# A new order of TensorE's work in the attention part and the first two experts of an xLSTM and mixture-of-experts kernel

## The chip, the cores and the metric

The kernel runs on one core of a Trainium2 chip. The metric is device time in microseconds of one execution; the time of the kernel before is the median of three runs.

## The reference

Three layers follow each other. The first is a gated linear attention (mLSTM) over 2 batches, 8 heads, 768 steps and a head size of 40. The second is a dense mixture of 4 experts over 1536 tokens, the third a top-1 mixture of 8 experts.

```python
# attention, per head and step t
C = f_stab * C + i_stab * outer(v_t, k_t)
n = f_stab * n + i_stab * k_t
y_t = sigmoid(o_t) * (C @ q_t) / max(abs(n @ q_t), 1.0)
# dense experts: x is (1536, 320), w1 (4, 320, 1024), w2 (4, 1024, 320)
p = domain_probs / (domain_probs.sum(-1, keepdims=True) + 1e-09)
out += p[:, e:e+1] * (np.maximum(x @ w1[e], 0.0) @ w2[e])     # for e in range(4)
# routed experts: one expert of 8 for each token, by the largest logit of x @ w_gate
out[i] = gate_w[i] * (np.maximum(disp @ w1[e], 0.0) @ w2[e])[pos[i]]
```

## The kernel before, in words

The sequence is cut into 12 chunks of 128 steps, 6 for each batch; chunk u gives token tile u of the experts. Chunks 0 to 3 run in float32. From chunk 4 on, operands are split into two float16 parts, high and low.

**Work items.** The attention and the first two experts (0 and 1) make up 48 + 24 items, and each has a place in one list, `SEQ`:

- `("S", u)`: the scores of chunk u (`scores32`, L1115, or `scores`, L1119). Ahead of it stand the broadcast of the chunk's maxima (L997) and the decay arguments (L1068 or L1075).
- `("B", u)`: the rest of chunk u: the product with the carried state (`inter`, L1205, L1215), with the values (`intra`, L1210, L1241), and the state's update (L1273, L1279).
- `("L", k, t)`: layer 1 of expert k on token tile t, in two halves of 32 matmuls (L644).
- `("M", k, t)`: layer 2 of the same, in two halves of 12 matmuls of 320 columns (L656).

**The planner.** `Sched` takes all operations of all engines with a guessed duration and their dependences. TensorE's operations have a due place, which for the items above is their index in `SEQ`. `urgency` turns these into latest starts, `starts` lays out a plan with all engines and the DMA queue, and `run` emits each engine's instructions in the plan's order. So the list sets not only TensorE's order: it moves the instructions of VectorE, ScalarE, GpSimd and the SP queue with it. On each engine the emitted order is kept.

**Fillers.** Where the plan has an idle stretch on TensorE in the first part (due place up to `FILLED = 45.0`), `gaps` puts matmuls on zeros there (`warm`, L416), 128x256 each; the plan's idle time after that place gets none.

**The way of one chunk from 4 on (`front`).** VectorE takes the maxima of q, k and v (L972), GpSimd reduces them over the partitions (L979), TensorE broadcasts the result into bank x3 (L997). VectorE reads that bank and makes power-of-two scales (`pow2_scale`, L442, L447, L452). ScalarE writes the high parts (L1027) and VectorE the low parts (L1033), q first, then k. SP issues a DMA transpose (L1039), and then the scores can run. After the scores VectorE multiplies by the decay (L1163), ScalarE rounds (L1176), GpSimd takes the rest (L1180), and `intra` can run.

**Other lines that the prediction names.** L665 is VectorE's low part of layer 1's output, L697 its sum into the output of a tile; L697 also sets free one of the two banks po0 and po1 that layer 2 writes. L589 and L594 split the weights of an expert into high and low float16 (`w_conv`), L551 broadcasts a weight maximum. L632 is the DMA transpose of a token tile, L422 any plain load.

Of the kernel before, what the change touches and what calls it, by code (L numbers as in the profile page):

```python
# [21 lines left out]
B, H, S, D = 2, 8, 768, 40  # L22
# [227 lines left out]
def xlstm_moe_kernel(ctx: ExitStack, tc: tile.TileContext, a, cap: int):  # L250
# [255 lines left out]
    wscale = lambda k, m: (wsm[:, k, m - 1, 8:9], wsm[:, k, m - 1, 9:10])  # L506

    SEQ = {x: i for i, x in enumerate((
 ("S", 0), ("B", 0), ("S", 1), ("B", 1), ("L", 0, 0), ("S", 2), ("L", 0, 1), ("M", 0, 1), ("B", 2), ("S", 3), ("L", 0, 2), ("B", 3), ("M", 0, 0), ("L", 1, 0), ("L", 1, 2), ("M", 1, 0), ("S", 4), ("M", 0, 2), ("L", 1, 1), ("B", 4), ("L", 0, 3), ("M", 1, 2), ("L", 1, 3), ("S", 5), ("L", 0, 4), ("S", 6), ("B", 5), ("M", 0, 4), ("L", 0, 5), ("S", 7), ("B", 6), ("M", 1, 1), ("L", 1, 5), ("B", 7), ("M", 0, 3), ("L", 1, 4), ("S", 8), ("B", 8), ("L", 0, 6), ("M", 0, 5), ("M", 1, 3), ("S", 9), ("B", 9), ("L", 0, 7), ("L", 0, 8), ("L", 1, 6), ("S", 10), ("M", 0, 7), ("L", 1, 9), ("M", 1, 6), ("M", 0, 8), ("M", 0, 6), ("L", 0, 10), ("B", 10), ("L", 0, 9), ("L", 1, 8), ("L", 1, 7), ("M", 0, 10), ("M", 1, 5), ("L", 1, 10), ("S", 11), ("M", 1, 8), ("M", 1, 4), ("B", 11), ("L", 0, 11), ("L", 1, 11), ("M", 1, 7), ("M", 0, 9), ("M", 1, 9), ("M", 1, 10), ("M", 1, 11), ("M", 0, 11),
    ))}  # L510
    at3 = NT * 10.0 + 50
    SPREAD_AT = {
# [1514 lines left out]
```

## Time and profile before

| | us |
|---|---|
| median of 3 runs (494.47 to 496.36) | 496.05 |
| the profiled execution, its own time | 495.52 |
| its span, first to last instruction | 493.8 |
| PE busy (96% of the span) | 475.5 |
| DVE busy (69%) | 340.6 |
| ACT busy (63%) | 311.9 |
| POOL busy (27%) | 131.7 |
| first matmul of expert 2, L644 with 512 columns | 196.07 |

The span has four parts: attention and experts 0 and 1 (to about 196 us), experts 2 and 3 with the routing, the routed experts, and a tail of scattered stores. The page sums engines over the whole span; the change acts on the first part, so its stretches have to be asked for apart.

### The profile page before, as it was taken

How to read it: one execution, taken by the hardware profiler on the slowest of the kernel's cores; microseconds unless marked ns; L12 is line 12 of the kernel's file. 1: busy time of each engine (PE TensorE's matmuls, PEld its weight loads, DVE VectorE, ACT ScalarE, POOL GpSimd, SP SyncE). 2: the span in 40 equal slices, each digit the busy share in tenths (PEclk: the TensorE clock that was granted, in tenths of full speed). 3: DMA queues.
4: the chain of work that ended last, by engine and by line, in shares of the span. 5: the costliest groups of instructions: out<-in, count | busy, mean ns of one | idle time of the engine just before them, and what ended most of it. 6: DMA issues, size and time to landing. Idle time of an engine off the chain costs nothing. (4 is left out here: it accounts for less than half of the span.)

```text
span 493.8 us, 13708 instructions
## 1 busy us (share of the span) xinstructions
PE 475.5 (96%) x5487; PEld 365.7 (74%) x5487; DVE 340.6 (69%) x972; ACT 311.9 (63%) x666; POOL 131.7 (27%) x243
## 2 busy tenths in 40 slices
PE   8999999999989899999999999999999999999994
PEld 6998978868868797886564746556564698888883
DVE  5898988799999834663968594879899982222120
ACT  1997979577687854856765568778879550322230
POOL 4751143665865410200010010000414111311111
PEclk9999999999999999999999999999999999999999
DMA  6996683354533796818686967628293545999200
GB/s 229 315 236 195 155 286 77 77 131 102 105 60 73 201 342 205 230 26 288 204 296 220 333 215 298 211 75 222 70 223 109 133 184 79 302 219 322 103 27 25
DMA packets 70772, 88.90 MB, mean 180 GB/s; under 512 B 48641, under 2 KB 56307, under 8 KB 70702
## 3 DMA queue, kind: packets, MB, share of 16 engines
q1 hardware_dynamic: 69502, 84.23, 59.4%
q0 software_dynamic: 1200, 3.73, 2.0%
q8 instruction: 45, 0.74, 0.6%
q14 instruction: 25, 0.20, 0.2%
HBM read 55.89 MB, written 21.70 MB: 157 GB/s over the span
## 5 line engine op out<-in xcount | busy, mean ns | idle before, releaser
L656 PEld LDWEIGHTS <-arena 128*128 128x128 f16 (+1 forms) x1416 | 136.4, 98 | 55.0 <-issue 3.2
L644 PEld LDWEIGHTS <-w 128*128 128x128 f16 x1792 | 97.3, 98 | 4.2 <-issue 2.8
L644 PE MATMUL ph<-xT,w 128*128 128x128 f16 (+3 forms) x1664 | 96.2, 217 | 1.2 <-DVE usm L442 0.9
L644 PEld LDWEIGHTS <-arena 128*128 128x128 f16 x960 | 64.2, 98 | 42.9 <-issue 1.8
L656 PE MATMUL po<-w,arena 128*128 128x320 f16 (+1 forms) x600 | 86.3, 299 | 2.1 <-DVE acc L697 1.3
L527 ACT ACTIVATE junk<-raw 128x512 bf16<-128x512 f32 (+1 forms) x105 | 69.6, 663 | 12.3 <-DMA raw<-in_moe_w_dram 10.8
L656 PE MATMUL po<-arena 128*128 128x320 f16 x504 | 71.3, 299 | 0.4 <-ACT arena L589 0.4
L665 DVE SCALAR_TENSOR_TENSOR arena<-ph,arena 128x512 f16<-128x512 f32 x80 | 54.5, 683 | 22.7 <-ACT arena L663 22.6
L644 PE MATMUL ph<-xT,arena 128*128 128x512 f16 (+4 forms) x512 | 66.7, 284 | 0.0
L589 ACT ACTIVATE w<-raw,wsm 128x640 f16<-128x640 f32 (+1 forms) x56 | 51.3, 961 | 18.1 <-DVE wsm L447 18.0
L663 ACT ACTIVATE arena<-ph 128x512 f16<-128x512 f32 x80 | 47.0, 587 | 22.7 <-PE ph L644 13.4
L594 DVE SCALAR_TENSOR_TENSOR w<-raw,wsm,w 128x640 f16<-128x640 f32 (+1 forms) x56 | 57.4, 1049 | 3.8 <-ACT w L589 3.7
L644 PE MATMUL x<-xT,arena 128*128 128x128 f16 (+4 forms) x448 | 52.2, 270 | 0.0
L545 POOL CROSS_LANE_REDUCE wsm<-wsm 128x1 f32<-128x6 f32 (+1 forms) x24 | 9.6, 402 | 107.9 <-ACT junk L527 78.7
L656 PE MATMUL x<-arena 128*128 128x320 f16 (+1 forms) x240 | 34.6, 299 | 0.1
L594 DVE SCALAR_TENSOR_TENSOR arena<-raw,wsm,arena 128x640 f16<-128x640 f32 (+1 forms) x28 | 30.4, 1103 | 3.0 <-ACT arena L589 3.0
L589 ACT ACTIVATE arena<-raw,wsm 128x640 f16<-128x640 f32 (+1 forms) x28 | 25.5, 955 | 3.6 <-DVE wsm L447 3.6
L685 POOL TENSOR_TENSOR cfs<-pw,invx 128x1 f32<-128x1 f32 x48 | 17.1, 388 | 37.1 <-DVE invx L452 29.8
L697 DVE SCALAR_TENSOR_TENSOR acc<-po,cfs,acc 128x320 f32<-128x320 f32 x30 | 16.4, 546 | 14.0 <-PE po L656 7.5
L1770 POOL DMA_INDIRECT out_dram<-acc,usm x13 | 12.7, 975 | 46.9 <-ACT acc L1767 45.0
L1180 POOL TENSOR_TENSOR arena<-arena 128x512 f16<-128x512 f32 x16 | 20.6, 1304 | 12.0 <-ACT arena L1176 12.0
L1457 POOL DMA_INDIRECT disp<-arena x12 | 13.8, 1150 | 34.5 <-ACT arena L663 17.3
(237 smaller groups left out, 649.3 us busy)
## 6 DMA issues: line engine op xcount, KB each, us to landing
raw<-in_moe_w_dram SPq DMA_DIRECT2D x36, 512.0 KB
raw<-in_moe_w_dram SPq DMA_DIRECT2D x24, 640.0 KB
ws<-w SPq DMA_DIRECT2D x8, 768.0 KB
ws<-w SPq DMA_DIRECT2D x8, 640.0 KB
arena<-in_att_dram SPq DMA_DIRECT2D x8, 492.0 KB
disp<-zero SPq DMA_DIRECT2D x1, 3936.0 KB
arena<-ws SPq DMA_DIRECT2D x4, 768.0 KB
arena<-ws SPq DMA_DIRECT2D x4, 640.0 KB
```

Source lines behind the costliest of these rows:

```text
L527: nc.scalar.activation(out=junk[:, 0:w], in_=raw[:, i * w:(i + 1) * w], func=AF.Abs, accum_out=am[:, i:i + 1])
L589: lambda sl=sl: nc.scalar.activation(out=wh[:, sl], in_=raw[:, sl], func=AF.Copy, scale=sc),
L594: lambda sl=sl: nc.vector.scalar_tensor_tensor(wl[:, sl], raw[:, sl], sc, wh[:, sl], ALU.mult, ALU.subtract),
L644: nc.tensor.matmul(out=out, lhsT=wb[wi][:, c, f * 128:(f + 1) * 128], rhs=rhs(xc), start=(i == 0), stop=(i == LAST))
L656: nc.tensor.matmul(out=po[0:n, 0:DM], lhsT=hs[:, f, sl], rhs=ws[:, f, :], start=(f == 0 and i == 0), stop=(f == NF - 1 and i == 2),)
L663: act(0.52, lambda: nc.scalar.activation(out=hh, in_=ph, func=AF.Relu), [kp] + ex, [kh])
L665: 0.6, lambda: nc.vector.scalar_tensor_tensor(hl, ph, 0.0, hh, ALU.max, ALU.subtract),
L685: 0.26, lambda: nc.gpsimd.tensor_tensor(cf, pw[:, t, k:k + 1], invx[:, t:t + 1], ALU.mult),
L697: lambda: nc.vector.scalar_tensor_tensor(acc[:, t], po[:, 0:DM], cf, acc[:, t], ALU.mult, ALU.add),
L1180: 1.3, lambda j=j: nc.gpsimd.tensor_tensor(Wl[:, j::2], pb[:, j::2], Wh[:, j::2], ALU.subtract),
L1457: sent[k("done")] = nc.gpsimd.indirect_dma_start(out=disp_t[t], out_offset=bass.IndirectOffsetOnAxis(ap=sli, axis=0), in_=R.bitcast(U32), ...
L1770: nc.gpsimd.indirect_dma_start(out=view_of(), out_offset=bass.IndirectOffsetOnAxis(ap=ix[0:n], axis=0), in_=acc[0:n, y], in_offset=None, b ...
```

## The change

The tuple in `SEQ` is replaced by another order of the same items. It begins so:

```diff
- ("S", 0), ("B", 0), ("S", 1), ("B", 1), ("L", 0, 0), ("S", 2), ("L", 0, 1), ("M", 0, 1), ("B", 2), ("S", 3),
+ ("S", 0), ("B", 0), ("S", 1), ("B", 1), ("L", 0, 0), ("L", 0, 1), ("S", 2), ("M", 0, 0), ("B", 2), ("L", 0, 2),
...
```

Nothing else is edited. In the emitted order no work is added or dropped except fillers: 64 of them before, 55 now. From where only expert 2's work is left, TensorE's order is the same.

The first place is VectorE behind the scores of chunk 11, where the weights of expert 2 are split (raw_86 and raw_87 are its raw weights, po_99 is bank po0, x_101 and x_102 are banks x0 and x1). Before:

```order
L594 SCALAR_TENSOR_TENSOR arena<-raw_86,wsm,arena 128x1024
L1325 RECIPROCAL usm<-usm 128x8
L594 SCALAR_TENSOR_TENSOR arena<-raw_86,wsm,arena 128x1024
L1337 SCALAR_TENSOR_TENSOR arena<-usm,arena 128x320
L1163 TENSOR_TENSOR arena<-x_101,arena 128x4x128
L1163 TENSOR_TENSOR arena<-x_102,arena 128x4x128
L665 SCALAR_TENSOR_TENSOR arena<-ph_98,arena 128x512
L440 TENSOR_SCALAR usm<-usm 128x1
L594 SCALAR_TENSOR_TENSOR arena<-raw_86,wsm,arena 128x1024
L442 TENSOR_SCALAR usm<-usm 128x1
L594 SCALAR_TENSOR_TENSOR arena<-raw_87,wsm,arena 128x640
L697 SCALAR_TENSOR_TENSOR acc<-po_99,cfs,acc 128x320
```

And the same place on VectorE with the change:

```order
L1163 TENSOR_TENSOR arena<-x_101,arena 128x4x128
L697 SCALAR_TENSOR_TENSOR acc<-po_99,cfs,acc 128x320
L1325 RECIPROCAL usm<-usm 128x8
L1163 TENSOR_TENSOR arena<-x_102,arena 128x4x128
L1337 SCALAR_TENSOR_TENSOR arena<-usm,arena 128x320
L665 SCALAR_TENSOR_TENSOR arena<-ph_97,arena 128x512
L594 SCALAR_TENSOR_TENSOR arena<-raw_86,wsm,arena 128x1024
L665 SCALAR_TENSOR_TENSOR arena<-ph_98,arena 128x512
L440 TENSOR_SCALAR usm<-usm 128x1
L594 SCALAR_TENSOR_TENSOR arena<-raw_86,wsm,arena 128x1024
```

L697 stood behind four splits of expert 2's weights and now stands ahead of all of them.

The second place is VectorE in chunk 9, between the read of its maxima and its last low part, L1033 (x_104 is bank x3, which the read of the maxima, L442, takes; in the old order that read and four more rows stand ahead of the first row here). Before:

```order
L452 TENSOR_SCALAR usm<-usm 128x1
L1009 TENSOR_SCALAR usm<-usm 128x1
L1003 TENSOR_SCALAR usm<-usm 128x1
L1005 TENSOR_SCALAR usm<-usm 128x1
L1151 SCALAR_TENSOR_TENSOR arena<-arena,usm 128x320
L1033 SCALAR_TENSOR_TENSOR arena<-arena,usm 128x8x40
L1163 TENSOR_TENSOR arena<-x_101,arena 128x4x128
L1163 TENSOR_TENSOR arena<-x_102,arena 128x4x128
L1229 TENSOR_TENSOR arena<-x_104,usm 128x328
L665 SCALAR_TENSOR_TENSOR arena<-ph_98,arena 128x512
L1033 SCALAR_TENSOR_TENSOR arena<-arena,usm 128x8x40
```

The same on VectorE with the change, from the read of the maxima on:

```order
L442 TENSOR_SCALAR usm<-x_104 128x4
L447 TENSOR_SCALAR usm<-usm 128x3
L452 TENSOR_SCALAR usm<-usm 128x3
L447 TENSOR_SCALAR usm<-usm 128x1
L452 TENSOR_SCALAR usm<-usm 128x1
L1009 TENSOR_SCALAR usm<-usm 128x1
L1003 TENSOR_SCALAR usm<-usm 128x1
L1005 TENSOR_SCALAR usm<-usm 128x1
L1033 SCALAR_TENSOR_TENSOR arena<-arena,usm 128x8x40
L1229 TENSOR_TENSOR arena<-x_104,usm 128x328
L1033 SCALAR_TENSOR_TENSOR arena<-arena,usm 128x8x40
```

Two L1163, one L1151 and two L665 (one of them among the four rows that are not shown) stood between and now stand elsewhere.

## Rows read from the trace of the kernel before

**Rows 1.** The page: busy time of PE, and the granted clock in 40 slices.
```profile
PE 475.5 (96%) x5487; PEld 365.7 (74%) x5487; DVE 340.6 (69%) x972; ACT 311.9 (63%) x666; POOL 131.7 (27%) x243
...
PEclk9999999999999999999999999999999999999999
```

**Rows 2.** Busy time by stretch: length, engines' busy us, granted clock, DMA share, GB/s.
```profile
12.00:197.00 185.00, 178.16 (x2466) 155.32 (x2466) 156.58 (x406) 141.34 (x317) 84.73 (x152) 1.00 0.63 171
...
196.00:250.00 54.00, 54.00 (x515) 39.22 (x514) 35.40 (x63) 37.02 (x74) 5.31 (x14) 1.00 0.62 193
```

**Rows 3.** PE's timeline, end of the first part: start us, length us, line, count.
```profile
181.59 7.31 PE L644 MATMUL ph<-xT,w 128*128 128x128 f16 x128
188.74 3.42 PE L656 MATMUL po<-w,arena 128*128 128x320 f16 x24
192.00 0.36 PE L1205 MATMUL x<-arena 120*128 120x41 f16 x8
192.21 0.76 PE L1210 MATMUL x<-arena 128*128 128x41 f16 x24
192.81 3.42 PE L656 MATMUL po<-w,arena 128*128 128x320 f16 x24
196.07 1.89 PE L644 MATMUL x<-xT,arena 128*128 128x512 f16 x8
```

**Rows 4.** PE's timeline: the first and the longest later run of fillers.
```profile
2.01 6.13 PE L416 MATMUL ph<-zero 128*128 128x256 f16 x31 [2.01 <-POOL zero L758]
...
27.49 2.58 PE L416 MATMUL ph<-zero 128*128 128x256 f16 x22
```

**Rows 5.** PE's timeline: its five longest waits of the first part, in brackets.
```profile
49.38 3.16 PE L656 MATMUL po<-w,arena 128*128 128x320 f16 x22 [0.81 <-DVE arena L665]
...
117.21 1.95 PE L644 MATMUL ph<-xT,w 128*128 128x128 f16 x32 [0.89 <-DVE usm L442]
...
138.58 0.37 PE L1205 MATMUL x<-arena 120*128 120x41 f16 x8 [1.13 <-ACT arena L1176]
...
148.40 0.62 PE L1119 MATMUL x<-arena 120*128 120x128 f16 x8 [1.11 <-DMA arena<-arena]
...
166.25 1.79 PE L656 MATMUL po<-w,arena 128*128 128x320 f16 x12 [1.27 <-DVE acc L697]
```

**Rows 6.** DVE's timeline, just ahead of that last wait's end.
```profile
164.02 1.71 DVE L594 SCALAR_TENSOR_TENSOR arena<-raw,wsm,arena 128x640 f16<-128x640 f32 x1
165.66 0.54 DVE L697 SCALAR_TENSOR_TENSOR acc<-po,cfs,acc 128x320 f32<-128x320 f32 x1
```

**Rows 7.** SP's timeline: the raw weights, and the transpose of chunk 4 behind them.
```profile
53.23 2.78 SPq L422 DMA_DIRECT2D raw<-in_moe_w_dram  x3
57.37 4.12 SPq L1039 DMA_TRANSPOSE arena<-arena  x1
```

**Rows 8.** PE's timeline: scores of chunk 4.
```profile
69.55 0.61 PE L1119 MATMUL x<-arena 120*128 120x128 f16 x8
```

**Rows 9.** The stretch from chunk 7's scores to chunk 11's, by engine.
```profile
109.30:157.50 48.20, 44.73 (x749) 39.06 (x747) 46.28 (x124) 35.55 (x73) 30.58 (x45) 1.00 0.43 83
```

**Rows 10.** The page: L665 (busy, mean ns, idle before).
```profile
L665 DVE SCALAR_TENSOR_TENSOR arena<-ph,arena 128x512 f16<-128x512 f32 x80 | 54.5, 683 | 22.7 <-ACT arena L663 22.6
```

**Rows 11.** PE's timeline: the scores of chunk 6, and the maxima of chunk 9.
```profile
100.11 0.62 PE L1119 MATMUL x<-arena 120*128 120x128 f16 x8 [0.22 <-DMA arena<-arena]
...
121.80 0.18 PE L997 MATMUL x<-usm,call 128*128 128x4 bf16 x1
```

**Rows 12.** SP's timeline: the transposes of chunks 6, 9 and 10.
```profile
96.40 1.60 SPq L1039 DMA_TRANSPOSE arena<-arena  x1
...
129.19 2.42 SPq L1039 DMA_TRANSPOSE arena<-arena  x1
...
142.35 2.00 SPq L1039 DMA_TRANSPOSE arena<-arena  x1
```

**Rows 13.** PE's timeline: a wait in the third part, on a weight maximum.
```profile
288.49 0.16 PE L551 MATMUL x<-wsm,call 128*128 128x1 bf16 x1 [1.07 <-POOL wsm L545]
```

More of the change, by code (lines that the diff above doesn't have):

```diff
@@ L508, in xlstm_moe_kernel @@
     SEQ = {x: i for i, x in enumerate((
- ("S", 0), ("B", 0), ("S", 1), ("B", 1), ("L", 0, 0), ("S", 2), ("L", 0, 1), ("M", 0, 1), ("B", 2), ("S", 3), ("L", 0, 2), ("B", 3), ("M", 0, 0), ("L", 1, 0), ("L", 1, 2), ("M", 1, 0), ("S", 4), ("M", 0, 2), ("L", 1, 1), ("B", 4), ("L", 0, 3), ("M", 1, 2), ("L", 1, 3), ("S", 5), ("L", 0, 4), ("S", 6), ("B", 5), ("M", 0, 4), ("L", 0, 5), ("S", 7), ("B", 6), ("M", 1, 1), ("L", 1, 5), ("B", 7), ("M", 0, 3), ("L", 1, 4), ("S", 8), ("B", 8), ("L", 0, 6), ("M", 0, 5), ("M", 1, 3), ("S", 9), ("B", 9), ("L", 0, 7), ("L", 0, 8), ("L", 1, 6), ("S", 10), ("M", 0, 7), ("L", 1, 9), ("M", 1, 6), ("M", 0, 8), ("M", 0, 6), ("L", 0, 10), ("B", 10), ("L", 0, 9), ("L", 1, 8), ("L", 1, 7), ("M", 0, 10), ("M", 1, 5), ("L", 1, 10), ("S", 11), ("M", 1, 8), ("M", 1, 4), ("B", 11), ("L", 0, 11), ("L", 1, 11), ("M", 1, 7), ("M", 0, 9), ("M", 1, 9), ("M", 1, 10), ("M", 1, 11), ("M", 0, 11),
+ ("S", 0), ("B", 0), ("S", 1), ("B", 1), ("L", 0, 0), ("L", 0, 1), ("S", 2), ("M", 0, 0), ("B", 2), ("L", 0, 2), ("S", 3), ("L", 1, 0), ("B", 3), ("S", 4), ("M", 0, 2), ("M", 1, 0), ("M", 0, 1), ("B", 4), ("L", 1, 1), ("S", 5), ("L", 1, 2), ("L", 1, 3), ("L", 0, 3), ("S", 6), ("B", 5), ("L", 0, 4), ("M", 1, 2), ("B", 6), ("M", 0, 3), ("L", 0, 5), ("M", 1, 1), ("M", 1, 3), ("S", 7), ("L", 1, 5), ("B", 7), ("S", 8), ("M", 0, 4), ("L", 1, 4), ("L", 0, 6), ("B", 8), ("M", 0, 5), ("L", 0, 7), ("S", 9), ("M", 0, 7), ("L", 0, 8), ("L", 1, 6), ("S", 10), ("L", 1, 9), ("M", 0, 6), ("L", 0, 10), ("L", 1, 8), ("L", 1, 7), ("L", 0, 9), ("L", 1, 10), ("M", 1, 7), ("B", 9), ("M", 1, 8), ("M", 1, 6), ("L", 0, 11), ("B", 10), ("M", 0, 9), ("L", 1, 11), ("M", 0, 8), ("M", 1, 5), ("M", 1, 10), ("S", 11), ("M", 1, 4), ("M", 1, 11), ("M", 0, 10), ("B", 11), ("M", 0, 11), ("M", 1, 9),
     ))}
```

## The prediction

> **What bounds the kernel now.** I read the page first, then busy time by stretch, then TensorE's own timeline, then the queues behind its waits. PE is busy for 96% of the span and the granted clock is full in every slice [rows 1], so time can come only from its idle time, its fillers, or work taken off it; the change takes no real work off. From 12 to 197 us PE is busy for 178.16 of 185 us, so 6.84 us are idle; from 196 us on it isn't idle at all for 54 us [rows 2]. At 196.07 us the first matmul of expert 2 starts with no wait [rows 3], and from where only expert 2's work is left PE's order is unchanged. So what the first part gains by then should move everything behind it by as much: the time is won or lost ahead of 196 us, in 6.84 us of waits plus fillers. Five waits make up 5.21 us of the 6.84 [rows 5]; the rest are pieces of 0.4 us or less.
>
> **Fillers.** There are 9 fewer. A run of 22 takes 2.58 us, 0.117 us each [rows 4], and PE goes from it straight to other work, so 9 x 0.117 = **1.05 us less**. The plan counted these stretches as idle. If the real work behind them isn't ready, the 1.05 us come back as waits, so the bounds are 0 and 1.05; I take all of it, since the earlier scores now stand in those places.
>
> **The wait at 166.25.** Layer 2 waits 1.27 us for the bank that L697 frees [rows 5]. L697 ends 0.05 us before, and had stood behind splits of expert 2's weights, the last of them 1.71 us long [rows 6]. In the new order L697 stands ahead of all those splits and between the two products of chunk 11. **1.27 us less**. The bounds are 0 (another L697 falls behind the same splits, which still have to run) and 1.27.
>
> **Up to the scores of chunk 4.** The wait of 0.81 us at 49.38 is layer 2 on the heels of its own layer 1: it waits for the low part, L665 [rows 5]. In the new order 14 small matmuls stand between the layer 1 just ahead and the next half of layer 2, 2.9 us by the durations below, and it goes. In exchange the scores of chunk 4 come early. They started at 69.55 [rows 8]. I add up PE's rows in the new order without any wait, with durations as in [rows 3]: 64 matmuls of layer 1 take 64 x 7.15/128 = 3.57 us, 12 of layer 2 take 1.63, and 24 small ones 0.6. By that sum they would start at 59.5. But their transpose is issued on SP behind the three loads of expert 2's first raw weights, which wait for expert 1's split, in both orders; the loads began at 53.23 and the transpose at 57.37, and SP spent 4.12 us on it [rows 7]. With both as now, and 3.7 us to land as in chunk 6 (below), it would be there after 61 us: a wait of up to 2 us. If the split comes 3 us earlier, as the earlier layer 1 allows, there is none. I take 0.4: **0.4 us less** in all (bounds 0.8 less and 1.2 more).
>
> **From chunk 7's scores to chunk 11's.** Here lie 3.47 us of PE's idle time: 48.20 less 44.73 [rows 9]. Three of the five waits are in it, at 117.21, 138.58 and 148.40 [rows 5]. But DVE is busy for 46.28 us of the same 48.20. In the new order this stretch holds 10 halves of layer 1 instead of 12, 9 halves of layer 2 instead of 8, and one state update more. On PE that is -2 x 1.79 + 1.63 + 0.6 = -1.35, so 43.4 us. On DVE two L665 of 0.68 go [rows 10], and the update's two sums and half an L697 come, some 0.55 each by L697 [rows 6], so it stays at 46.3. With DVE full the stretch lasts 46.3 us and PE idles for 2.9; with DVE's idle time as now it lasts 48.2 and PE idles for 4.8. The present 3.5 lies between, and I take **no change** (bounds 3.5 less, if DVE's work moves out of the stretch, and 1.3 more). The waits need not stay at the same places. In chunk 9 PE sees the maxima at 121.80 and SP issues the transpose at 129.19, 7.4 us later [rows 11, 12]. From issue to the scores it took 3.7 us in chunk 6 and 6.05 in chunk 10, whose scores waited [rows 5, 11, 12]. So 11.1 to 13.4 us are needed. In the new order I count only 8.6 us of PE work between maxima and scores in chunks 8 and 9, 10.1 in 10 and 9.1 in 11. What speaks for it all the same is the second excerpt of the order: two L1163, two L665 and L1151, some 3.1 us at 0.5 to 0.7 each, no longer stand between, so that chunk 9 needs 8.0 to 10.3.
>
> **The sum.** -1.05 - 1.27 - 0.4 + 0 = -2.7 us. The profiled execution took 495.52, so it would take 492.8; the median of the runs shown is 0.53 above it, so I predict **493.3 us**. On other engines the moves lie beside PE. That cover is thin on DVE, as the stretch above shows, and late on ACT and SP only where the waits above say so.
>
> A rule of the Trainium skill speaks against an order that bets on short waits. The longest wait after the start is 1.27 us, and the granted clock stays 1.00 in all the stretches shown [rows 2, 5, 9]. The rule, in "TensorE: Matmul & The Clock Gate", section "HAM oscillation — how this bites in real kernels", is that a TensorE left idle between bursts falls back to half clock and has to earn the full one again. This trace shows no such fall behind a wait, so the sum has no term for it; it is the last rival.
>
> **The rivals.** About 0.5%, 2.5 us, is what a measurement of this kernel can tell from no change, so "faster" is below 493.6.
>
> 1. **The waits go as well.** Chunks 4 to 7 start earlier, where DVE has slack, and DVE's work leaves the full stretch. Then its 3.5 us go too: -6.2, or 489.9. For it: the shorter way from maxima to transpose in chunk 9. Against it: the DVE sum.
> 2. **DVE gives it back.** DVE keeps its idle time, so PE idles 1.3 us more between chunks 7 and 11, the 1.27 us find another place behind the splits, and chunk 4 eats what the first terms gave: -1.05 + 1.3 = +0.2, or 496.3 by the median. A wait such as that at 288.49, for a weight maximum that comes at its own pace, would grow by part of what comes earlier [rows 13], and leads to the same. For it: DVE's 46.28 of 48.20 us.
> 3. **The transposes come too late, and it is slower.** If chunks 8 to 11 need 12.3 us from maxima to scores, the middle of 11.1 and 13.4, each waits by its shortfall: 3.7 + 3.7 + 2.2 + 3.2 = 12.8 in place of 3.5, so -2.7 + 9.3 = +6.6, or 502.7. It is slower by more than 2.5 us once they need more than 11.3 on average: (3.47 + 2.7 + 2.5)/4 = 2.2 above the mean cover of 9.1. For it: all three measured pieces. Against it: DVE's queue is shorter just there.
> 4. **The clock falls behind a long wait.** The 31 first fillers took 6.13 us, 0.198 each against 0.117 later [rows 4], though the page gives the full clock for them too. A fall with such a stretch of slow matmuls would cost 31 x 0.081 = 2.5 us on top of the wait that brings it on: with one of 3 us behind the forecast, 498.8.
>
> That the order doesn't change as the table says is excluded: the emitted instructions show it.
>
> **How the numbers follow.** The forecast, from 4 us less to 1.3 less, gets 0.51, and its middle lies at the bound of what can be told: 0.27 of it faster, 0.24 the same. The first rival gets 0.18, all faster. The second gets 0.20, the same. The third gets 0.09 and the fourth 0.02, slower. So faster 0.45, the same 0.44, slower 0.11. Range: **489.0 to 497.5**. It takes in the first two rivals with about 1 us beyond each, and leaves out the third, the fourth and the far ends of the bounds.
>
> **What would show it.** In the new profile, right would be: 55 fillers; the first 512-column L644 at about 193.4 instead of 196.07; no wait of L656 on L697 near 160 us; chunk 4's scores at 59 to 62; PE idle for 3 to 4 us between chunks 7 and 11 with DVE above 95% there; later waits on weight maxima still near 1.8 us in all. It would be wrong if the 512-column L644 starts early but the span's end doesn't follow (the weights' own pace), if L1119 in chunks 8 to 11 waits for its transpose by over 2 us each (third rival), or if waits after chunk 7 come to under 1.5 us (first rival).

## The result and the profile after

The changed kernel took 497.18 us (median of 21 executions, 493.97 to 500.82), the kernel before 494.43 beside it: a ratio of 1.0064 [1.0046, 1.0083]. It is slower: by **3.2 us** by the ratio, by 2.75 by the medians. The forecast was 2.7 us faster. Medians are of all executions; ratios leave out those over 1.5% above their kernel's fastest. The profiled execution took 498.33 us, with a span of 496.5.

In the rows PE is TensorE (PEld its weight loads), DVE VectorE, ACT ScalarE, POOL GpSimd and SP the queue of DMA issues. The granted clock is the share of TensorE's full clock that it got. The page of the changed kernel, busy time and granted clock:

```profile
PE 477.4 (96%) x5478; PEld 367.0 (74%) x5478; DVE 341.4 (69%) x972; ACT 313.2 (63%) x666; POOL 126.2 (25%) x243
...
PEclk9989989999999999999999999999999999999999
```

Against [rows 1] the clock line is new: two dips, in the third and the sixth slice. Busy time by stretch dates them (columns as in [rows 2]; the number after the brackets of POOL is the granted clock):

```profile
12.00:197.00 185.00, 176.00 (x2431) 153.91 (x2430) 153.56 (x399) 138.50 (x312) 79.82 (x152) 0.98 0.64 166
34.00:36.00 2.00, 2.00 (x21) 1.92 (x19) 2.00 (x8) 2.00 (x7) 1.77 (x4) 0.63 0.88 239
36.00:38.00 2.00, 2.00 (x21) 1.78 (x20) 2.00 (x4) 1.48 (x3) 1.80 (x2) 0.52 1.04 231
65.00:67.00 2.00, 2.00 (x14) 1.39 (x15) 1.68 (x4) 1.76 (x5) 1.12 (x2) 0.56 0.70 271
67.00:69.00 2.00, 2.00 (x11) 1.13 (x9) 0.60 (x1) 0.37 (x2) 0.76 (x2) 0.59 0.39 108
250.00:300.00 50.00, 50.00 (x303) 29.05 (x301) 40.02 (x73) 31.67 (x59) 4.35 (x9) 1.00 0.81 278
```

PE is idle for 9.00 us of the 185 where it was 6.84 [rows 2], and part of its busy time is slow. A clock near 0.5 is the lower level, 1.2 GHz of 2.4.

PE's timeline shows the first dip. Ahead of it stand 15 fillers where before there were 27:

```profile
26.91 0.83 PE L416 MATMUL ph<-zero 128*128 128x256 f16 x6
28.32 1.12 PE L1279 MATMUL x<-arena 128*128 128x82 f32 x8 [0.58 <-DVE arena L1222]
29.27 1.15 PE L416 MATMUL ph<-zero 128*128 128x256 f16 x9
...
34.40 2.02 PE L1115 MATMUL x<-arena 40*128 40x128 f32 x16
36.34 4.48 PE L644 MATMUL ph<-xT,w 128*128 128x128 f16 x64
40.66 0.82 PE L416 MATMUL po<-zero 128*128 128x256 f16 x6
```

From 34.40 to 40.66 are 6.26 us. At full clock the same took 4.66: 1.09 for the scores and 3.57 for the layer 1. So this fall costs **1.60 us**. The second dip, and the longer waits up to chunk 7's scores:

```profile
64.92 0.79 PE L1119 MATMUL x<-arena 120*128 120x128 f16 x8 [2.14 <-DMA arena<-arena]
65.51 4.96 PE L656 MATMUL po<-w,arena 128*128 128x320 f16 x24
70.31 0.17 PE L997 MATMUL x<-usm,call 128*128 128x4 bf16 x1
...
77.65 0.76 PE L1273 MATMUL x<-arena 128*128 128x41 f16 x24 [0.99 <-DVE usm L447]
...
86.44 1.53 PE L656 MATMUL po<-w,arena 128*128 128x320 f16 x10 [1.92 <-DVE arena L665]
...
92.75 3.73 PE L644 MATMUL ph<-xT,w 128*128 128x128 f16 x64 [0.88 <-DVE arena L665]
...
113.12 1.96 PE L644 MATMUL ph<-xT,w 128*128 128x128 f16 x32 [1.00 <-DMA xT<-arena]
...
119.98 0.61 PE L1119 MATMUL x<-arena 120*128 120x128 f16 x8
```

Chunk 4's scores wait 2.14 us for their transpose, and the 24 matmuls behind them take 4.80 us, start to start, in place of 3.26: a second fall, **1.54 us**. Four more waits of about a microsecond or two follow. SP's timeline has the cause of the first wait, and DVE's that of the wait at 86.44:

```profile
54.08 2.72 SPq L422 DMA_DIRECT2D raw<-in_moe_w_dram  x3
58.10 3.40 SPq L1039 DMA_TRANSPOSE arena<-arena  x1
```

```profile
84.61 1.18 DVE L972 TENSOR_REDUCE usm<-arena 128x3 f32<-128x984 f32 x1 [2.03 <-DMA arena<-in_att_dram]
85.71 0.68 DVE L665 SCALAR_TENSOR_TENSOR arena<-ph,arena 128x512 f16<-128x512 f32 x1
```

The three weight loads and the transpose stand on SP 0.8 and 0.7 us later than before [rows 7], not earlier, and the scores start 6.8 us after the transpose's issue. DVE waits for a load at chunk 8's maxima (L972); the eviction that PE needs (L665, which reads layer 1's bank) is queued behind them.

Behind chunk 7 the order does better than forecast. Layer 2 follows chunk 11's scores without the wait of 1.27 us in [rows 5]; the first matmul of expert 2, the last row, answers to the last of [rows 3]:

```profile
162.85 0.61 PE L1119 MATMUL x<-arena 120*128 120x128 f16 x8
163.29 1.79 PE L656 MATMUL po<-w,arena 128*128 128x320 f16 x12
164.92 1.95 PE L644 MATMUL ph<-xT,w 128*128 128x128 f16 x32
...
199.95 1.24 PE L644 MATMUL x<-xT,arena 128*128 128x512 f16 x5
```

And the stretch from chunk 7's scores to chunk 11's, which answers to [rows 9]:

```profile
119.98:162.85 42.87, 42.35 (x699) 36.40 (x697) 38.83 (x109) 32.45 (x66) 21.67 (x32) 1.00 0.42 76
```

To account for the whole first part I added up PE's rows of either order at full clock and without waits (from the first L832, at 10.49 and 10.43 us, on; durations start to start as in the prediction) and set the measured times beside them. The excess is what was taken over the rows alone, by waits or by a slow clock; all in us, counted from the span's start:

| stretch | before: took, rows alone, excess | changed: took, rows alone, excess |
|---|---|---|
| to chunk 4's scores | 69.55, 67.34, 2.21 | 64.92, 59.45, 5.47 |
| to chunk 7's scores | 39.77, 38.19, 1.58 | 55.06, 46.94, 8.12 |
| to chunk 11's scores | 48.21, 43.38, 4.83 | 42.87, 41.44, 1.43 |
| to expert 2 | 38.54, 37.14, 1.40 | 37.10, 37.15, -0.05 |
| sum | 196.07, 186.05, 10.02 | 199.95, 184.98, 14.97 |

So the change is -1.07 of work, +9.8 of excess up to chunk 7 (3.14 of it the slow clock) and -4.85 of excess behind it: expert 2 starts 3.88 us later. The span ends 2.7 us later; 1.07 of the 1.2 us between is the wait at 288.49 [rows 13], which is gone.

### The profile page after: what moved, and what is told of

It is laid out like the page before. It is cut to its first block, busy times and chain, and to the rows that moved or that the text cites. A ratio compares the mean times of both kernels' runs of the same rounds, so it can differ in the third digit from the quotient of the medians.

```text
span 496.5 us, 13694 instructions
## 1 busy us (share of the span) xinstructions
PE 477.4 (96%) x5478; PEld 367.0 (74%) x5478; DVE 341.4 (69%) x972; ACT 313.2 (63%) x666; POOL 126.2 (25%) x243
## 3 DMA queue, kind: packets, MB, share of 16 engines
q0 software_dynamic: 1200, 3.73, 2.2%
## 5 line engine op out<-in xcount | busy, mean ns | idle before, releaser
L656 PE MATMUL po<-w,arena 128*128 128x320 f16 (+1 forms) x600 | 88.6, 302 | 1.9 <-DVE arena L665 1.9
L665 DVE SCALAR_TENSOR_TENSOR arena<-ph,arena 128x512 f16<-128x512 f32 x80 | 54.7, 684 | 22.6 <-ACT arena L663 22.4
L594 DVE SCALAR_TENSOR_TENSOR arena<-raw,wsm,arena 128x640 f16<-128x640 f32 (+1 forms) x28 | 29.4, 1065 | 2.6 <-ACT arena L589 2.6
L697 DVE SCALAR_TENSOR_TENSOR acc<-po,cfs,acc 128x320 f32<-128x320 f32 x30 | 16.3, 545 | 13.0 <-PE po L656 5.9
L1764 DVE SCALAR_TENSOR_TENSOR arena<-ph,arena 128x512 f16<-128x512 f32 (+1 forms) x10 | 6.5, 651 | 25.0 <-ACT arena L1759 19.2
```

Source lines behind the costliest of these rows:

```text
L594: lambda sl=sl: nc.vector.scalar_tensor_tensor(wl[:, sl], raw[:, sl], sc, wh[:, sl], ALU.mult, ALU.subtract),
L656: nc.tensor.matmul(out=po[0:n, 0:DM], lhsT=hs[:, f, sl], rhs=ws[:, f, :], start=(f == 0 and i == 0), stop=(f == NF - 1 and i == 2),)
L665: 0.6, lambda: nc.vector.scalar_tensor_tensor(hl, ph, 0.0, hh, ALU.max, ALU.subtract),
L697: lambda: nc.vector.scalar_tensor_tensor(acc[:, t], po[:, 0:DM], cf, acc[:, t], ALU.mult, ALU.add),
```

## The experiments

Three questions: does the loss lie ahead of chunk 7 and the gain behind it, and can they be had apart? Is it the clock? Is it one queue or one instruction? Ratios are to the kernel before, run beside each on the same chip.

### Cuts of the order

The list is the old one up to a chunk's scores and the new one behind it, or the reverse; items that one half has done are left out of the other. Where the two meet, for the first pair:

```diff
- old: ... ("S", 7), ("B", 6), ("M", 1, 1), ("L", 1, 5), ("B", 7), ("M", 0, 3), ...
+ e5:  ... ("S", 7), ("B", 6), ("M", 0, 3), ("M", 1, 1), ("M", 1, 3), ("L", 1, 5), ...
- new: ... ("S", 7), ("L", 1, 5), ("B", 7), ("S", 8), ("M", 0, 4), ...
+ e6:  ... ("S", 7), ("M", 0, 4), ("L", 1, 5), ("B", 7), ("L", 1, 4), ("S", 8), ...
```

> TensorE's old order up to and with chunk 7's scores, the new order for all that follows. Theory A (the new order loses between chunk 3 and chunk 7's scores and gains behind them): chunk 7's scores stand near 109.3 us as before; from there to expert 2's first product the changed kernel took 79.97 us where the kernel before took 86.75, so expert 2 starts near 189.5 (before 196.07) and the time is 6 us under before less some 1 us that the later experts give back: near 489 us, ratio 0.989. Theory B (the gain behind chunk 7 came only from the delay ahead of it, in which VectorE got ahead): VectorE is full again between chunks 7 and 11, expert 2 starts within 1 us of 196, and the time is that of before, ratio 0.998 to 1.003.

> The other half: the new order up to and with chunk 7's scores, the old order for what follows. Theory A: chunk 7's scores stand near 120 us as in the changed kernel, the old order then takes its 86.75 us, expert 2 starts near 206 and the time is some 5 us above the changed kernel's: near 502, ratio 1.016. Theory B: the delay ahead of chunk 7 gives VectorE its lead here too, chunk 7 to expert 2 takes some 80 us, expert 2 starts near 200 and the time is the changed kernel's, ratio 1.005 to 1.008.

And at chunk 4, and with the old order in the middle alone:

```diff
- new: ... ("B", 3), ("S", 4), ("M", 0, 2), ("M", 1, 0), ("M", 0, 1), ("B", 4), ...
+ e10: ... ("M", 1, 0), ("S", 4), ("M", 0, 2), ("B", 4), ("L", 1, 1), ("S", 5), ...
+ e11: ... ("B", 3), ("S", 4), ("M", 0, 1), ("L", 1, 2), ("M", 1, 0), ("M", 0, 2), ...
+ e12: as e11 up to ("S", 7), and then as the new order
```

> TensorE's old order up to and with chunk 4's scores, the new order behind them. Theory stretch (the waits ahead of chunk 7 belong to the new order between chunks 4 and 7): TensorE waits 4 to 6 us between the scores of chunks 4 and 7, expert 2 starts near 197, time near 495, ratio 1.000 to 1.004. Theory early (they follow from chunk 4 being taken up 8 us of work earlier, before its data are there): at most 2 us of waits there, expert 2 near 193, time near 491, ratio 0.992 to 0.996.

> The other cut: the new order up to and with chunk 4's scores, the old order behind them. Theory early: chunk 4's scores wait 2 us for their transpose, 4 us or more of waits follow up to chunk 7, and the old order's 4.7 us behind chunk 7 come on top: ratio 1.010 or more. Theory stretch: the 2 us wait stays, but under 2 us follow up to chunk 7: ratio 1.002 to 1.006.

> The changed kernel with the old order only from chunk 4's scores up to chunk 7's (what the old order had ahead of chunk 4 and the new one has not yet done stands first there). Theory pair (neither the new order up to chunk 4 nor the new order from 4 to 7 is costly by itself; the two together take chunks 4 to 7 up before their data are there): TensorE waits under 3 us between the two scores, chunk 7's scores stand near 109, expert 2 starts near 192.5, time 3 us under before, ratio 0.994 to 0.997. Theory early (the new order up to chunk 4 costs by itself, by the wait for chunk 4's transpose and the clock behind it): ratio 0.999 to 1.004.

Measured, sorted by ratio (o: old order, n: new, in the stretches to chunk 4, from 4 to 7, and behind 7; the last four columns are of one profile each, in us: the start of chunk 7's scores and of expert 2, and PE's idle time in between):

| kernel | order | median us | ratio [95%] | chunk 7 | expert 2 | PE idle 4 to 7 | PE idle 7 to expert 2 |
|---|---|---|---|---|---|---|---|
| e10 | o n n | 489.48 | 0.9934 [0.9904, 0.9964] | 112.96 | 192.71 | 2.13 | 0.48 |
| e5 | o o n | 491.65 | 0.9947 [0.9919, 0.9975] | 108.49 | 193.34 | 1.67 | 1.10 |
| e12 | n o n | 493.92 | 0.9995 [0.9967, 1.0022] | 110.20 | 195.14 | 1.87 | 1.33 |
| before | o o o | 492.77 to 494.43 | 1 | 109.32 | 196.07 | 0.84 | 4.75 |
| e11 | n o o | 493.34 | 1.0012 [0.9984, 1.0039] | 108.73 | 194.49 | 0.25 | 3.95 |
| changed | n n n | 497.18 | 1.0064 [1.0046, 1.0083] | 119.98 | 199.95 | 5.44 | 0.52 |
| e6 | n n o | 505.03 | 1.0127 [1.0048, 1.0206] | 114.81 | 199.37 | 3.95 | 4.85 |

The starts carry an offset: already the first L832 stands at 9.21 us in e5, 9.78 in e10 and 10.49 before. The idle times don't.

Loss and gain come apart. **e5 and e10 beat both kernels.** The new order behind chunk 7 gains in every pair that differs by it alone: 0.0053 from o o o to o o n, 0.0017 from n o o to n o n, 0.0063 from n n o to n n n (the last two within the intervals). The last column shows it better: PE idles 3.95 to 4.85 us there with the old order and 0.48 to 1.33 with the new. e5's rows by stretch, chunk 7's scores to chunk 11's and on to expert 2:

```profile
108.49:155.75 47.26, 46.47 (x760) 39.99 (x760) 44.40 (x120) 32.39 (x71) 26.29 (x42) 1.00 0.43 83
155.75:193.34 37.59, 37.28 (x495) 32.10 (x495) 23.73 (x49) 25.32 (x50) 8.52 (x22) 1.00 0.78 248
```

PE idles 0.79 and 0.31 us there; before it was 3.47 [rows 9] and 1.27 [rows 5]. Chunk 7 was on time in e5, so the gain doesn't need the delay ahead of it, as theory B had it. My 489 was too low for another reason: I carried over the changed kernel's 79.97 us, but with the old head e5 has more work left behind chunk 7 (83.75 us of busy PE, against 42.35 + 37.10 = 79.45).

Ahead of chunk 7 it takes both halves to bring the waits: between the scores of chunks 4 and 7 PE idles 5.44 us in the changed kernel and 3.95 in e6, and 0.25 to 2.13 in the five others. In e11 and e12 the old order's layer 2 and layer 1 items, left over, stand right behind chunk 4's scores and cover the chunks' chains. In the changed kernel little such work is left, and PE waits for a scale, two evictions and a DMA transpose (77.65 to 113.12 above). The times agree less well. The new order from 4 to 7 costs nothing behind the old start (e10 is no slower than e5), but the new start costs 0.0012 from o o o to n o o, 0.0048 from o o n to n o n and 0.0130 from o n n to n n n. So it isn't free with the old middle either, though the first is within the interval. Part of that is fillers: old starts have 27 early ones, new ones 15. With 29 the changed kernel comes to 0.9997 (e14, below), still 0.0063 above e10.

e12 fell between its two theories: its waits from chunk 4 to 7 are under 3 us as "pair" said, its time is at the low end of "early". e6 loses further behind expert 2, with a wait of 2.35 us on a weight maximum (L551) at 310.87, so its 1.0127 (by the medians 1.022) isn't all of the first part.

### The clock: fillers

Four kernels changed fillers alone. e1 puts 18 just ahead of chunk 4's scores, e2 lengthens those planned between 20 and 30 us, e9 does both, and e4 takes the 27 of that place out of the kernel before.

```diff
+         for i, (b, us) in list(fill.items()):
+             if 20.0 < start[i] < 30.0:
+                 fill[i] = (b, us + 0.7)
...
+         if u == 4:
+             sch.more[len(sch.ops)] = ("x0", 2.0)
...
+         fill = {i: x for i, x in fill.items() if not 20.0 < start[i] < 30.0}
```

> The changed kernel with 18 more fillers (2.1 us) on TensorE just ahead of the scores of chunk 4, where it waits 2.14 us for their transpose, and where the granted clock is 0.56 from 65 to 69 us behind the wait. Theory A (the half clock behind that wait is paid in full): the 24 matmuls of layer 2 behind the scores take 3.26 us from start to start instead of 4.80, everything behind moves up by 1.5 us, and the time is 1 to 1.7 us below the changed kernel's 497.2. Theory B (DVE and the loads set the pace of chunks 5 to 7, so that what comes earlier waits): the clock is back at 1.00 from 65 to 69 us, but the scores of chunk 7 start within 0.5 us of 119.98 and the time is that of the changed kernel within 0.5 us.

> The changed kernel with the two filler runs ahead of chunk 1's update and chunk 2's B lengthened by 0.7 us each (27 or 28 fillers there instead of 15; the kernel before had 27 there). In the changed kernel the granted clock is 0.63 and 0.52 from 34 to 38 us, which cost some 1.6 us (the scores of chunk 3 take 1.94 us from start to start instead of 1.09, the 64 matmuls of layer 1 behind them 4.32 instead of 3.57). Theory A (fewer fillers let the clock fall): clock 1.00 from 34 to 38 us, the first layer 1 no later than 36.6 although 12 to 14 fillers more run, and 0.5 to 1.5 us less in all. Rival (the clock fell for another reason, such as the narrow float32 matmuls there): it falls as before, and the time rises by 0.3 to 0.9 us.

> The changed kernel with both sets of fillers: the 12 or 13 more between 20 and 30 us and the 18 just ahead of chunk 4's scores. No wait goes. If the clock's falls at 34 to 38 us and behind the wait for chunk 4's transposes are what costs (theory clock): both go, some 3.1 us by the profile of the changed kernel (1.6 and 1.5), time near 493.5, ratio 0.997 to 1.001, and fewer slow executions than with either set alone. If the fillers only take up waiting time and the clock's falls cost little (rival): ratio 1.004 to 1.007 as the changed kernel.

> The kernel before without its 27 fillers between 27 and 32 us (2.58 and 0.71 us), nothing else changed. Theory A (these fillers hold the clock): the granted clock falls to about half for some 4 us near 30 to 40 us, as it does in the changed kernel, and the time rises by 1 to 2.5 us. Rival (they only fill idle time): the clock stays at 1.00 and the time is the same within 0.5 us.

Measured: e1 1.0033 [1.0007, 1.006], e2 1.0003 [0.9976, 1.0031], e9 1.0024 [0.9995, 1.0053], and e4, the kernel before without them, 1.0033 [1.0011, 1.0055]. e4's profile shows the wait that the fillers had covered, and the granted clock behind it:

```profile
29.53 1.27 PE L1216 MATMUL x<-arena 128*128 128x82 f32 x8 [2.42 <-POOL wsm L546]
```

```profile
34.00:36.00 2.00, 2.00 (x22) 2.00 (x20) 1.09 (x3) 0.02 (x1) 1.50 (x3) 0.50 1.02 242
```

Fillers that take no wait away brought the changed kernel up to 3 us. But these runs didn't stand beside its 1.0064, and in most profiles with 15 early fillers the clock stayed full near 36 us. So three kernels were set side by side on one chip: the changed one as it is (15 early fillers), with 14 more as in e2, and with none (the last line of the diff above).

> The changed kernel as it is (15 fillers between 26 and 31 us), beside the next two on the same chip, so that the three differ by fillers alone. Both theories: ratio 1.003 to 1.008.

> The changed kernel with 14 more fillers there, 29 in all. Theory clock (each stretch that stands empty ahead of 34 us costs by the granted clock behind it): 2 to 3 us less than with 15 fillers. Rival (the fall at 34 to 38 us that the changed kernel's profile shows comes in few executions; what the runs so far differ by is the chip): within 1 us of the run with 15.

> The changed kernel without the 15 fillers there. Theory clock: the clock falls near 30 to 38 us in most executions, 1.5 us or more on top of the run with 15. Rival: within 1 us of it, and the profile shows a full clock or a fall that costs no time at chunk 4's scores.

| early fillers | median us | ratio [95%] |
|---|---|---|
| none (e15) | 502.54 | 1.0173 [1.013, 1.0216] |
| 15 (e13, the changed kernel) | 496.90 | 1.0073 [1.0036, 1.0109] |
| 29 (e14) | 494.30 | 0.9997 [0.9967, 1.0026] |

Each lot of 15 or 14 fillers, 1.75 or 1.64 us of zeros, is worth more than itself: 5.6 us and then 2.6. For the first lot the theory of the clock holds. e15's timeline shows how:

```profile
28.34 1.12 PE L1280 MATMUL x<-arena 128*128 128x82 f32 x8 [1.33 <-DVE arena L1223]
30.31 1.20 PE L1216 MATMUL x<-arena 128*128 128x82 f32 x8 [0.85 <-DVE arena L1290]
31.59 1.90 PE L1242 MATMUL x<-arena 128*128 128x41 f32 x8
...
36.97 2.08 PE L1116 MATMUL x<-arena 40*128 40x128 f32 x16
38.99 4.88 PE L645 MATMUL ph<-xT,w 128*128 128x128 f16 x64
```

The two waits are about as long as what stood there with 15 (6 fillers of 0.70 us and a wait of 0.58, then 9 fillers of 1.05), but behind them the granted clock is 0.50 to 0.53 from 31 to 38 us. In e13's profile, at full clock, the same stretch reads:

```profile
31.87 1.08 PE L1241 MATMUL x<-arena 128*128 128x41 f32 x8
...
34.74 1.16 PE L1115 MATMUL x<-arena 40*128 40x128 f32 x16
35.84 3.75 PE L644 MATMUL ph<-xT,w 128*128 128x128 f16 x64
```

From the first L1242 to the layer 1 it is 7.40 us against 3.97, and the layer 1 takes 4.88 against 3.75: 4.6 us. The absent fillers gave no time back: the first L1242 starts at 31.59 us in e15 and 31.87 in e13, whose first L832 is 0.32 us later too.

The second lot is not explained by this. The mean granted clock of every execution was measured. At half clock TensorE loses half of the time, so an execution lost some (1 - clock) x time to the clock directly. That is an estimate and rather too high: it takes in time in which TensorE waited anyway, and a fall behind the last matmul. The median clocks are 0.981 with none, 0.9935 with 15, 0.995 with 29 and 0.996 for the kernel before, which makes 9.5, 3.2, 2.5 and 2.0 us. From 15 to none that is 6.3 us more, enough for the 5.6 measured. In e4 it is 0.987 against 0.997 beside it, 5.0 us, where its ratio shows 1.6; waits elsewhere took up part of the rest, for apart from the two waits that the fillers had covered (2.42 and 0.35 us) PE idles 4.41 us from 12 us to expert 2, where it was 6.84. But from 29 to 15 it is only 0.7 of the 2.6 us; what the rest is, no run shows.

The profiles say the same. Of eight with 15 early fillers and the new order up to chunk 4, one, the changed kernel's, shows a fall near 36 us, and a fall in one of eight, at 1.60 us each, doesn't make 2.6 us. Most of them are executions below their kernel's median (e13's took 495.64 of 496.90), and slower ones do have a lower clock: in e13 the four from 498.84 to 500.3 us have 0.991 on average and the seven below them 0.996, some 2 us by the estimate, where they are 4 us slower. Covering chunk 4's wait as well brought nothing more: e9 is no faster than e2 and e14.

### One queue, one instruction

e3 takes expert 2's three weight loads on SP behind chunk 4's transpose. e7 takes chunk 8's maxima on DVE behind one eviction (and one L1163), and e8 joins that to e2.

```diff
+     sch.behind = [([("raw", 2, 1, j) for j in range(3)], ("turn", 4))]
...
+         moved = [self.max8]
+         for i in order[at:end + 1]:
+             if ops[i][3] & set(moved):
+                 moved.append(i)
+         order[at:end + 1] = [i for i in order[at:end + 1] if i not in moved] + moved
```

> The changed kernel with one edit of SP's queue: the three loads of expert 2's first raw weights are issued behind chunk 4's transpose instead of ahead of it. All other queues keep their order. Theory A (the transpose is late because 1.5 MB of raw weights are ahead of it): it lands some 3 us earlier, the wait of 2.14 us at chunk 4's scores falls below 0.5, the clock stays at 1.00 from 65 to 69 us, and the scores of chunk 5 start 3 to 3.7 us before 81.83. In the end 1.5 to 3.5 us less than the changed kernel. Theory B (DVE's and ScalarE's work sets the time of the transpose, or chunks 5 to 7 wait for other things): the scores of chunk 4 start less than 1 us earlier, or the gain at chunk 5 is gone by the scores of chunk 7 at 119.98.

> The changed kernel; on VectorE alone chunk 8's maximum (L972) goes behind the eviction L665 and the piece of L1163 that stood right behind it. In the changed kernel VectorE stood idle 2.03 us there for chunk 8's load, and TensorE waited 1.92 us for that eviction. If this wait is on the path (theory A): it goes, chunk 7's scores come 1.9 us earlier (near 118), and the time falls by some 1.9 us, ratio 1.002 to 1.003. If chunk 7's scores are bound by other chains (theory C: the xT transposes and the loads on SP, which do not move): later waits grow by what this one loses, and the time stays at ratio 1.005 to 1.007.

> The changed kernel with the 12 or 13 more fillers between 20 and 30 us (ratio 1.0003 alone) and with chunk 8's maximum moved as in the run before. If the two losses add: 494.0 less 1.9, near 492, ratio 0.996. If the second only moves to the next wait: ratio near 1.000.

Measured: e3 1.0054 [1.0024, 1.0085]; e7 1.0014 [0.9977, 1.0052], by its medians, 496.26 and 494.04, 1.0045; e8 1.0013 [0.9986, 1.0039]. In e3 chunk 4's wait shrinks from 2.14 to 0.77 us, and waits of 1.18, 1.81 and 1.26 us stand behind it: the time hardly moves. In e7 the wait at 86.44 is gone, and two behind it, 0.88 and 1.00 in the changed kernel, have grown:

```profile
87.49 3.73 PE L654 MATMUL ph<-xT,w 128*128 128x128 f16 x64 [1.65 <-DVE arena L675]
...
107.75 1.96 PE L654 MATMUL ph<-xT,w 128*128 128x128 f16 x32 [1.22 <-DMA xT<-arena]
```

So part of the wait moves to the next eviction, as theory C said, but not all: PE's idle time from chunk 4's scores to chunk 7's is 4.19 us, where it was 5.44 in the changed kernel and 5.32 in e13. The time, which allows both theories, is inconclusive. e8 is no faster than e2, so the two edits don't add up. Neither edit alone frees chunks 4 to 7. e8's profile has the clearest wait with a fall behind it: 2.88 us, and then 64 matmuls of layer 1 that take 5.36 us where 3.73 is usual:

```profile
91.13 5.36 PE L657 MATMUL ph<-xT,w 128*128 128x128 f16 x64 [2.88 <-DVE arena L678]
```

## Why the prediction was wrong

- **Fillers (-1.05): failed.** As work they went, as the -1.07 of the table shows. The step "their cost is their own length" and its bounds of 0 and 1.05 were wrong: 14 put back are worth 2.6 us, and taking the other 15 out costs 5.6. The clock explains the 5.6 and 0.7 of the 2.6; the rest of the 2.6 stays open. The sentence "this trace shows no such fall behind a wait, so the sum has no term for it" took the absence of a fall in a kernel that was filled against it as evidence for one that isn't. The fourth rival had the mechanism, with a chance of 0.02 and a wait of 3 us ahead of the fall; the falls came behind shorter ones. Its price of 2.5 us was that of 31 slow fillers; the two falls in the changed kernel's profile cost 1.60 and 1.54 each.
- **Up to chunk 4 (-0.4): failed.** The wait of 0.81 us went, as forecast (26 small matmuls, 2.74 us, stand there, not the 14 that I counted). But the excess of the stretch grew by 3.26 us, 1.60 of them the clock near 36 us. I counted on the split of expert 1's weights, and so on SP's loads, coming up to 3 us earlier; they came no earlier, and the 3.7 us from the transpose's issue to the scores, taken from chunk 6, were 6.8. My upper bound of 2 us for that wait was nearly what it measured, 2.14.
- **Chunks 4 to 7: no term, and the largest loss**, +6.54 us of excess, 1.54 by the clock. I costed the places where the kernel before waited; this stretch had hardly any waits there, so I left it out. With chunk 4 taken up 8 us of work earlier and 47 us of work up to chunk 7 in place of 38, the chains behind it (loads, maxima, scales, transposes) became late next. e10, e11 and e12 show that these waits need the two parts together.
- **Chunks 7 to 11 (0): failed in the other direction**, -3.40. "With DVE full" was wrong: DVE's 38.83 us in the new stretch are 7.5 fewer, not the same, and between chunks 4 and 7 it has 44.80 where it had 34.26. In e5 DVE is busy for 44.40 of 47.26 us, nearly as full as the 46.28 of 48.20 before, and PE idles 0.79 us in place of 3.47: PE's idle time didn't follow from DVE's busy share. On PE the state update that I counted as one more isn't there (96 of L1273 in both stretches), so its rows fall by 1.94 us, not 1.35. This is the first rival: DVE's work left the stretch, and the waits went.
- **The wait at 166.25 (-1.27): held.** It is gone, also in e5, whose idle time there is 0.31 us.
- **Transposes of chunks 8 to 11 (third rival):** it didn't happen; no L1119 there waits for its transpose. The later waits on weight maxima, which I expected to stay near 1.8 us, shrank: the one at 288.49 is gone.

The Trainium skill's rule that I cited ("TensorE: Matmul & The Clock Gate", section "HAM oscillation — how this bites in real kernels": left idle between bursts, TensorE falls back to half clock) bore on this change after all. The traces agree in kind: in the changed kernel, in e4, e8 and e15 granted clocks of 0.50 to 0.63 stand behind waits of 0.85 to 2.88 us or, at 34 us in the changed kernel, behind shorter ones. What the falls cost is told above; they are part of the loss and not all of it.

## What to carry to other kernels

When an order is changed, recompute every stretch, not only those in which the old order waits: write down when each chunk's data can be there, and how much independent work stands ahead of its first use. Matmuls on zeros that look like free savings may be holding the clock; before counting their absence as a gain, run the kernel without them, and look at the granted clock of many executions. A new order that loses as a whole may be good in one half: cut it at a place where both have the same work behind them and try the halves.

## What the runs showed of the hardware

The clock fell behind idle time that I had thought too short to matter: 1.33 and 0.85 us in e15, among narrow float32 matmuls. In the changed kernel's profile it fell at 34 us behind waits of 0.17 and 0.58 us only; e13, the same kernel, has the same two waits and no fall. Even e10, the fastest kernel, has a fall in its profile, behind a wait of 1.24 us (0.62 from 76 to 78 us). And the same wait doesn't bring the fall each time: behind chunk 4's scores it came after 2.14 us (changed), 1.99 (e8) and 2.30 (e15), and not after 2.75 (e13), 2.58 (e2) or 2.07 (e6). The rows of e13 (the same 24 matmuls took 4.96 us in the changed kernel's profile above):

```profile
64.29 0.62 PE L1119 MATMUL x<-arena 120*128 120x128 f16 x8 [2.75 <-DMA arena<-arena]
64.75 3.42 PE L656 MATMUL po<-w,arena 128*128 128x320 f16 x24
```

So a single profile at full clock doesn't tell that the kernel keeps it in every execution.
